# Decoding all float64 weight chunks by way of a PSUM bank, earlier, in a kernel whose order a planner writes

## The chip, the cores and the metric

One core of one Trainium2 chip runs the kernel. The metric is the device time of one launch in microseconds (us). Matmuls run on TensorE (PE), whose clock is granted at one of two levels, 1.2 or 2.4 GHz; VectorE (DVE), ScalarE (ACT) and GpSimd (POOL) do the rest; SyncE (SP) issues all transfers.

## The reference

Causal attention with a decay bias, then two layers of which the first takes a maximum over three projections and the second applies a rational function:

```python
scores = scale * q @ k.T            # 4 batches x 8 heads, 576 positions, 64 wide
bias = -(cum[:, None] - cum[None, :])          # cum: running sum of max(s, 0)
scores = where(causal, -1e9, scores + minimum(bias, 0))
attn = softmax(scores)              # divided by (sum + 1e-9)
x = (attn @ v) as (2304, 512)
h = maximum(maximum(x @ w1, x @ w2), x @ w3)   # 512 -> 768
x = h @ w_out                                  # 768 -> 512
h = x @ w_in2                                  # 512 -> 2048
g = (a0 + a1*h + a2*h^2 + a3*h^3) / (1 + |b0|*|h| + |b1|*h^2 + 1e-6)
return g @ w_out2                              # 2048 -> 512
```

The weights w1, w2, w3, w_out, w_in2 and w_out2 are float64 in memory; the rest is float32.

## The kernel before

Every float32 product is made of three products of float32r halves, so each operand is split into a high part and a remainder (`split`, `minus`: L238 is a copy or cast, L241 a subtract, whatever they work on).

**Attention.** The 32 heads go as 16 pairs (`pr` 0 to 15). For a pair, the K and Q loads (`raw_k`, `raw_q`) are transposed on PE for pairs 0 to 2 (L438) and on DVE after that (`T_k`, `T_q`, L453) and split into `qkT`. `scores` (L502) fills PSUM banks with scores of five row tiles P0 to P4; DVE adds the mask and takes the row minima (L529), ACT the exponentials with their row sums (L537), DVE the reciprocals (`norm`, L555 and L556), and GpSimd or ACT scale the tiles by them (L546, L544). The "flips" (`flip`, L605 and L610) transpose the normalised tiles on PE into banks, which are copied to `PT`; from pair 6 on DVE transposes tile P4 instead (L585) and ACT and GpSimd place it by 16 small copies (`regroup`). `values` (L671) multiplies by V, and the result is split into `x` (cast L238, remainder L684).

**First layer.** When the four pairs of a batch are done, `experts` multiplies its x by w1, w2, w3: 36 "expert groups" a batch, each 12 matmuls of 128x288 on PE (L187) into one bank, and keeps their maximum (`hs`, L797). These groups are the work with which PE is filled while the attention of later pairs waits for other engines. From about 348 us on, PE has only experts and the second layer left (L187, L1022).

**Weights.** A chunk of 128x512 float64 weights (512 KB, `raww`) is turned into float32 on DVE by integer steps (`decode`): L713 shifts the high word, L716 adds the sign, L718 the top bits of the low word. Without `bank` all three write the SBUF tile `wx`; with it the first two work in a bank of PSUM, which L718 reads, and the bank is held from L713 to L718. There are 18 chunks of w1, w2, w3, which are then split into `w13`, 36 of the other weights that are written back to memory as float32 (`spill`), and two that are decoded directly later. Before, the first six go by a bank and 48 of the others by `wx`.

**The order.** Nothing waits for a scheduler on the chip: `Plan` takes every step with a rank, a planned cost on each engine that may do it, its inputs and the banks it takes, and simulates the engines; each time it issues the step that can start first, so the sequence on each engine, and the engine of a step that has a choice (`anyof`), come out of planned times. `SLACK` is added to the planned time of a PE step whose input comes from another engine, from rank 4 on; `wire` plans the transfers.

Of the kernel before, what the change touches and what calls it, by code (L numbers as in the profile page):

```python
# [24 lines left out]
class Plan:  # L25
# [38 lines left out]
    def issue(self):  # L64
        steps = self.steps
        left = [len(s[3]) for s in steps]
        after = [[] for _ in steps]
        for n, s in enumerate(steps):
            for p in s[3]:
                after[p].append(n)  # L70
        end = [0.0] * len(steps)
        est = [0.0] * len(steps)
        engine = {e: self.BEGIN.get(e, 0.0) for s in steps for e in s[0]}
        ready = {e: set() for e in engine}
        for n, s in enumerate(steps):
            if not left[n]:
                for e in s[0]:
                    ready[e].add(n)
        idle = [(0.0, b) for b in self.banks]
        wire = 0.0  # L80
        mode = None
        for _ in steps:
            best = None
            for e, cand in ready.items():
                t = engine[e]
                mine = None
                for n in cand:
                    engs, rank, _, _, take, _, kb, new, price = steps[n]
                    start = max(t, est[n], wire - self.AHEAD if kb else 0.0)
                    if take:  # L90
                        if len(idle) < len(take):
                            continue
                        start = max(start, idle[len(take) - 1][0])
                    if len(engs) > 1 and any(max(engine[o], est[n]) + c * price[o] < start + engs[e] * price[e] for o, c in engs.items() if o != e):
                        continue
                    key = (max(start, t + 0.1), rank + (self.STAY if new and new != mode else 0.0), n)
                    if mine is None or key < mine[0]:
                        mine = (key, start)
                if mine is not None and (best is None or mine[1] < best[0]):
                    best = (mine[1], mine[0][2], e)  # L100
            start, n, e = best
            engs, _, fn, _, take, free, kb, new, _ = steps[n]
            cost = engs[e]
            if new:
                cost += self.TURN if new != mode else 0.0
                mode = new
            for o in engs:
                ready[o].discard(n)
            for h in take:
                h.bank = idle.pop(0)[1]  # L110
            fn(e) if len(engs) > 1 else fn()
            engine[e] = start + cost
            if kb:
                wire = max(wire, start + cost) + kb / (190.0 if wire < 70.0 else 225.0)
                end[n] = wire + 2.0
            else:
                end[n] = start + cost
            lag = self.LAG[e]
            for h in free:
                idle.append((end[n] + lag, h.bank))  # L120
                idle.sort(key=lambda x: x[0])
            for m in after[n]:
                if "ctl" in steps[m][0]:
                    at = start
                else:
                    at = end[n] + ((1.0 if steps[n][1] > 16.0 else 0.0) if kb else self.SAME[e] if list(steps[m][0]) == [e] else lag)
                est[m] = max(est[m], at + (self.SLACK if steps[m][1] > 4.0 and "pe" in steps[m][0] and e not in ("pe", "ctl") else 0.0))
                left[m] -= 1
                if not left[m]:
                    for o in steps[m][0]:  # L130
                        ready[o].add(m)
        return max(end)
# [3 lines left out]
def kernel(  # L136
# [58 lines left out]
    def open_pool(name, **kw):  # L195
        g = tc.tile_pool(name=name, bufs=1, reuse_waits="tile", **kw)
        open_pools[name] = g
        return g.__enter__()
# [17 lines left out]
    def ve(rank, n, fn, reads=(), writes=(), free=(), cost=None):  # L216
        return plan.add({"dve": cost or c_dve(n)}, rank, fn, reads, writes, (), free)
# [13 lines left out]
    def anyof(engs, rank, fn, reads=(), writes=(), free=(), pre=(), price=None):  # L231

        if len(engs) == 1:
            return plan.add(engs, rank, lambda: fn(*engs), reads, writes, (), free, pre=pre)
        return plan.add(engs, rank, fn, reads, writes, (), free, pre=pre, price=price)

    def copy(e, out, in_):
        nc.scalar.copy(out=out, in_=in_) if e == "act" else (nc.vector if e == "dve" else nc.gpsimd).tensor_copy(out, in_)  # L238
# [11 lines left out]
    at = open_pool("at", side="right")  # L250
    n_w = [0]

    def wslot(name, shape=(128, 2, 512)):
        return wp.tile(list(shape), F32R, tag="w", bufs=3 * KF1, name=name)

    def wkey():
        n_w[0] += 1
        return ("w", (n_w[0] - 1) % (3 * KF1))
# [47 lines left out]
    raww = [p1.tile([128, 512, 2], U32, name="raww0"), at.tile([128, 512, 2], U32, name="raww1")]  # L306
    wx = [p1.tile([128, 512], U32, name=f"wx{i}") for i in range(2)]
# [275 lines left out]
    def regroup(pr, rank):  # L583
        for y in range(2):
            ve(rank, 0, lambda y=y: nc.vector.transpose(out=P4[:, :, y], in_=P4[:, :, y]), (), [("P", y, 4)], cost=0.83)  # L585
        for a in range(4):
            for g in range(4):
                anyof({"act": 0.42, "pool": 0.5}, rank + 0.05, lambda e, a=a, g=g: copy(
                    e, PTT[32 * g:32 * g + 32, 1792 + 320 * a:2112 + 320 * a], P[4][32 * a:32 * a + 32, 320 * g:320 * g + 320]),
                      [("P", y, 4) for y in range(2)], [("PT", 8 + 4 * a + g)], (), val[pr - 1] if pr - 1 not in DV else ())  # L590

# [98 lines left out]
    def cols(w, fc):  # L690

        return w.bitcast(U32).rearrange("(k p) f -> p k f", p=128)[:, :, 256 * fc:256 * fc + 256]
# [12 lines left out]
    def decode(rank, raw, x, kraw, kx, bank=False):  # L705


        hold = Hold()

        def way():  # L710
            return hold.bank.bitcast(U32) if bank else x()

        plan.add({"dve": 0.6 if bank else 0.4}, rank, lambda: nc.vector.tensor_scalar(  # L713
            way(), raw()[:, :, 1], 5, 2, ALU.logical_shift_left, ALU.logical_shift_right),
            [kraw], [kx], [hold] if bank else ())
        ve(rank, 0, lambda: nc.vector.scalar_tensor_tensor(  # L716
            way(), raw()[:, :, 1], 0xC0000000, way(), ALU.bitwise_and, ALU.bitwise_or), [kraw], [kx], cost=0.5 if bank else 0.65)
        ve(rank, 0, lambda: nc.vector.scalar_tensor_tensor(  # L718
            x(), raw()[:, :, 0], 29, way(), ALU.logical_shift_right, ALU.bitwise_or), [kraw], [kx],
            [hold] if bank else (), cost=0.5 if bank else 0.65)  # L720
# [21 lines left out]
    def m_rank(b, x):  # L742


        return 4 * b + 4.9 + 4.0 * x / NG
# [5 lines left out]
    def weights():  # L751
        for i in range(3 * KF1):
            fc, m = divmod(i, 3)
            rank = m_rank(0, 6 * fc) - 1.1
            r = raww[i % 2]
            key = w13_key[m, fc] = wkey()

            def new(m=m, fc=fc):
                w13[m, fc] = wslot(f"w13_{fc}_{m}")

            plan.add({"ctl": 0.0}, rank, new, (), [key, "w order"])
            load_raw(rank, r, cols((w1, w2, w3)[m], fc), ("raww", i % 2), e_dma[:4])
            decode(rank, lambda r=r: r, lambda i=i: wx[i % 2], ("raww", i % 2), ("wx", i % 2), i < 6)
            split(rank, lambda i=i: wx[i % 2].bitcast(F32), lambda m=m, fc=fc: w13[m, fc], ("wx", i % 2), key, PR(0 if i < 6 else 9))
        for i, (kind, x) in enumerate(spill):
            rank = S0 + (S1 - S0) * i / len(spill)
            r = raww[i % 2]
            load_raw(rank - 0.3, r, w2_src(kind, x), ("raww", i % 2))
            decode(rank, lambda r=r: r, lambda i=i: wx[i % 2], ("raww", i % 2), ("wx", i % 2))
            dm(rank, 256, w2_dram[i], wx[i % 2].bitcast(F32), [("wx", i % 2)], [("spill", i)])  # L770


# [34 lines left out]
    for pr in range(NP):  # L807
# [12 lines left out]
        if pr in DV:  # L820
            regroup(pr, pr + 0.3)
# [4 lines left out]
        if pr == 0:  # L826
            weights()
# [87 lines left out]
    for i, (_, kind, x) in enumerate(need[:20 + 2 * KF1]):  # L915
        rank = NP + 0.5 + 4.5 * i / 32
# [129 lines left out]
    for c in range(len(chunks) + 4):  # L1046
        n, fc = chunks[min(c, len(chunks) - 1)]
        r = R0 + c
# [49 lines left out]
```

## Time and profile before

| | |
|---|---|
| three timed runs | 891.7 us median (889.71 to 892.25) |
| profiled execution | 893.76 us, of which the span from first to last instruction is 892.0 us |
| busy share of the span | PE 98%, DVE 76%, ACT 60%, GpSimd 44% |
| mean granted clock of PE | 0.99 |

The shares are means over stages with different limits: attention runs until about 348 us, with experts in between, and after that there are matmuls alone. A wait counts only where PE has nothing else to do.

### The profile page before, as it was taken

What the parts mean: (1) busy time and instruction counts of PE and PEld (TensorE: products, weight loads), DVE (VectorE), ACT (ScalarE), POOL (GpSimd) and SP (SyncE); (2) the same over time, 40 slices, a digit from 0 to 9 for tenths busy, and PEclk for the clock granted to TensorE, in tenths of its full rate; (3) what the DMA queues carried; (4) which work ended last, traced back from release to release, by engine and by line L of the source; (5) the groups of instructions that cost most, each with busy time, mean ns of one, the idle gap of its engine ahead of it and who ended that gap; (6) DMA issues with size and microseconds to landing.
All of it is one profiled execution on the core that took longest, in us unless ns stands there. A gap on an engine that the chain in (4) does not pass through costs nothing.

```text
span 892.0 us, 17600 instructions
## 1 busy us (share of the span) xinstructions
PE 872.2 (98%) x6308; PEld 811.2 (91%) x6308; DVE 678.0 (76%) x1488; ACT 532.3 (60%) x1249; POOL 394.9 (44%) x506
## 2 busy tenths in 40 slices
PE   8899899999999999999999999999999999999998
PEld 8789888899999999999999999999999999999997
DVE  8999898878889975764897588478758856874875
ACT  7796476666766654322765576476547647663664
POOL 4465486545444533002853453254335415531432
PEclk9989999999999999999999999999999999999999
DMA  6887757767776754735200010020001002000000
GB/s 167 191 210 195 211 154 210 205 192 220 221 227 195 210 189 152 258 104 146 71 1 1 28 62 1 27 63 1 1 27 64 1 21 68 1 1 1 36 2 35
DMA packets 80664, 93.01 MB, mean 104 GB/s; under 512 B 33792, under 2 KB 61952, under 8 KB 80544
## 3 DMA queue, kind: packets, MB, share of 16 engines
q1 hardware_dynamic: 80576, 91.89, 35.8%
q8 instruction: 49, 0.80, 0.4%
q14 instruction: 39, 0.32, 0.1%
HBM read 69.96 MB, written 21.82 MB: 103 GB/s over the span
## 4 chain that ended last, share of the span: by engine, by line
PE 77%; DVE 8%; POOL 7%; ACT 2%; issue 2%; DMA 2%; SPq 1%; POOLq 0%; DVEq 0%; ACTq 0%
PE bank L187 46%; PE bank L1022 22%; POOL PT L238 4%; PE bank L671 3%; PE bank L610 3%; DVE P L529 2%; PE bank L502 2%; POOL P L546 2%; ACT P L537 1%; DVE P L585 1%; DMA raw_q<-in_q_dram 1%; DVE wx L716 1%; SPq L244 1%; DVE wx L718 1%; PE bank L605 1%
## 5 line engine op out<-in xcount | busy, mean ns | idle before, releaser
L187 PE MATMUL bank<-x,w 128*128 128x288 f32 x1728 | 244.9, 299 | 2.0 <-DVE small L529 2.0
L187 PEld LDWEIGHTS bank<-x,w 128*128 128x128 f32 x1728 | 233.8, 190 | 6.6 <-DVE small L529 2.3
L1022 PE MATMUL bank<-ws,g 128*128 128x512 f32 x864 | 215.5, 393 | 0.0
L187 PE MATMUL bank<-x,ws 128*128 128x384 f32 x1008 | 190.2, 336 | 0.0
L1022 PEld LDWEIGHTS bank<-ws,g 128*128 128x128 f32 x864 | 160.9, 188 | 29.4 <-DVE g L1002 0.2
L187 PEld LDWEIGHTS bank<-x,ws 128*128 128x128 f32 x1008 | 178.2, 188 | 7.1
L978 POOL TENSOR_SCALAR q<-a,cf 128x384 f32<-128x384 f32 x96 | 65.8, 686 | 182.1 <-ACT a L973 181.6
L537 ACT ACTIVATE P<-P,small 128x320 f32<-128x320 f32 (+5 forms) x160 | 89.3, 563 | 25.4 <-DVE small L529 24.8
L980 POOL TENSOR_TENSOR q<-q,a 128x384 f32<-128x384 f32 x96 | 97.8, 1019 | 8.0
L546 POOL TENSOR_SCALAR P<-P,small 128x448 f32<-128x448 f32 (+5 forms) x78 | 57.7, 752 | 96.9 <-ACT P L537 80.0
L995 DVE SCALAR_TENSOR_TENSOR q<-q,cf,bank 128x384 f32<-128x384 f32 x96 | 58.8, 613 | 49.1 <-ACT bank L993 45.9
L241 POOL TENSOR_TENSOR h<-h 128x384 fp32r<-128x384 f32 x30 | 31.1, 1058 | 115.2 <-ACT h L889 100.9
L1001 ACT CAST g<-t 128x384 fp32r<-128x384 f32 x96 | 49.4, 514 | 51.6 <-DVE t L999 51.6
L990 ACT ACTIVATE a<-q,cf 128x384 f32<-128x384 f32 x96 | 59.3, 617 | 28.4 <-POOL q L980 27.4
L187 PE MATMUL bank<-h,ws 128*128 128x384 f32 x432 | 75.9, 336 | 0.0
L187 PEld LDWEIGHTS bank<-h,ws 128*128 128x128 f32 x432 | 75.0, 188 | 0.5
L973 ACT ACTIVATE a<-bank 128x384 f32<-128x384 f32 x96 | 46.9, 489 | 40.8 <-PE bank L187 40.3
L981 DVE TENSOR_TENSOR t<-bank,t 128x384 f32<-128x384 f32 x96 | 53.0, 552 | 21.1 <-ACT t L975 21.1
L797 DVE TENSOR_TENSOR hs<-bank,hs 128x288 f32<-128x288 f32 x96 | 43.1, 449 | 31.3 <-PE bank L187 29.9
L975 ACT ACTIVATE t<-bank,cf 128x384 f32<-128x384 f32 x96 | 64.0, 666 | 0.0
L982 DVE SCALAR_TENSOR_TENSOR t<-t,cf,bank 128x384 f32<-128x384 f32 x96 | 58.8, 613 | 2.4
L999 DVE SCALAR_TENSOR_TENSOR t<-t,cf,bank 128x384 f32<-128x384 f32 x96 | 58.8, 612 | 2.5
(112 smaller groups left out, 1328.8 us busy)
## 6 DMA issues: line engine op xcount, KB each, us to landing
raww<-in_moe_w_out_dram SPq DMA_DIRECT2D x22, 512.0 KB
raww<-in_moe_w_dram SPq DMA_DIRECT2D x18, 512.0 KB
w_dram<-wx SPq DMA_DIRECT2D x36, 256.0 KB
ws<-w_dram SPq DMA_DIRECT2D x36, 256.0 KB
raw_k<-in_k_dram SPq DMA_DIRECT2D x52, 140.0 KB
raw_q<-in_q_dram SPq DMA_DIRECT2D x52, 140.0 KB
raww<-in_moe_w_in_dram SPq DMA_DIRECT2D x14, 512.0 KB
h_dram<-hs SPq DMA_DIRECT2D x48, 144.0 KB
```

What stands on the lines that cost most here:

```text
L187: nc.tensor.matmul(ps, l, r, start=begin and i == 0, stop=end and i == len(seq) - 1)
L537: ac(rank + 0.04, 0, lambda Pi=Pi, m=m, nr=nr: nc.scalar.activation(out=Pi, in_=Pi, func=ACTF.Exp, bias=sm[0:nr, 0, m:m + 1], scale=-1.0, ...
L546: (nc.vector if e == "dve" else nc.gpsimd).tensor_scalar(t, t, c, 0.0, ALU.mult, ALU.add)
L975: ac(rank, 0, lambda: nc.scalar.activation(out=t2[kt], in_=hold.bank[:, 0:TB], func=ACTF.Identity, scale=cf[:, 3:4], bias=cf[:, 2:3]), [(" ...
L978: po(rank, 0, lambda: nc.gpsimd.tensor_scalar(t2[kq], t2[ka], cf[:, 5:6], cf[:, 4:5], ALU.mult, ALU.add), [ka, "cf4"], [kq], cost=0.75)
L980: po(rank, 0, lambda: nc.gpsimd.tensor_tensor(t2[kq], t2[kq], t2[ka], ALU.mult), [ka], [kq], cost=0.97)
L981: ve(rank, TB, lambda: nc.vector.tensor_tensor(t2[kt], hold.bank[:, 0:TB], t2[kt], ALU.mult), [("hp", ci)], [kt])
L982: ve(rank, 0, lambda: nc.vector.scalar_tensor_tensor(t2[kt], t2[kt], cf[:, 1:2], hold.bank[:, 0:TB], ALU.add, ALU.mult), [("hp", ci), ("h ...
L990: ac(rank, 0, lambda: nc.scalar.activation(out=t2[a], in_=t2[qq], func=ACTF.Ln, bias=cf[:, 6:7], scale=1.0), [kq, "cf6"], [ka], cost=0.52)
L995: ve(rank, 0, lambda: nc.vector.scalar_tensor_tensor(t2[qq], t2[qq], cf[:, 6:7], hold.bank[:, 0:TB], ALU.add, ALU.mult), [kr], [kq], cost= ...
L999: ve(rank, 0, lambda: nc.vector.scalar_tensor_tensor(t2[t], t2[t], cf[:, 0:1], hold.bank[:, 0:TB], ALU.add, ALU.mult), [kr, turn], [kt], f ...
L1022: nc.tensor.matmul(hold.bank, t2[kg][:, ga, ts], w2["o2", fc][:, wb, :], start=(fc == 0 and x == 0), stop=(fc == KF2 - 1 and x == 2))
```

## The change

All chunks but the two direct ones are decoded by way of a bank; the chunks of the first layer get a rank 1.6 instead of 1.1 pairs ahead of their use; a PE step that needs a GpSimd result is planned 0.35 us later than one that needs any other; a regroup copy on ACT is planned at 0.47 us instead of 0.42, and the planned rate of transfers rises at 85 us instead of 70.

```diff
--- before.py
+++ after.py
@@ -111,7 +111,7 @@
             fn(e) if len(engs) > 1 else fn()
             engine[e] = start + cost
             if kb:
-                wire = max(wire, start + cost) + kb / (190.0 if wire < 70.0 else 225.0)
+                wire = max(wire, start + cost) + kb / (190.0 if wire < 85.0 else 225.0)
                 end[n] = wire + 2.0
             else:
                 end[n] = start + cost
@@ -124,7 +124,7 @@
                     at = start
                 else:
                     at = end[n] + ((1.0 if steps[n][1] > 16.0 else 0.0) if kb else self.SAME[e] if list(steps[m][0]) == [e] else lag)
-                est[m] = max(est[m], at + (self.SLACK if steps[m][1] > 4.0 and "pe" in steps[m][0] and e not in ("pe", "ctl") else 0.0))
+                est[m] = max(est[m], at + ((self.SLACK + 0.35 if e == "pool" else self.SLACK) if steps[m][1] > 4.0 and "pe" in steps[m][0] and e not in ("pe", "ctl") else 0.0))
                 left[m] -= 1
                 if not left[m]:
                     for o in steps[m][0]:
@@ -585,7 +585,7 @@
             ve(rank, 0, lambda y=y: nc.vector.transpose(out=P4[:, :, y], in_=P4[:, :, y]), (), [("P", y, 4)], cost=0.83)
         for a in range(4):
             for g in range(4):
-                anyof({"act": 0.42, "pool": 0.5}, rank + 0.05, lambda e, a=a, g=g: copy(
+                anyof({"act": 0.47, "pool": 0.5}, rank + 0.05, lambda e, a=a, g=g: copy(
                     e, PTT[32 * g:32 * g + 32, 1792 + 320 * a:2112 + 320 * a], P[4][32 * a:32 * a + 32, 320 * g:320 * g + 320]),
                       [("P", y, 4) for y in range(2)], [("PT", 8 + 4 * a + g)], (), val[pr - 1] if pr - 1 not in DV else ())
 
@@ -751,7 +751,7 @@
     def weights():
         for i in range(3 * KF1):
             fc, m = divmod(i, 3)
-            rank = m_rank(0, 6 * fc) - 1.1
+            rank = m_rank(0, 6 * fc) - 1.6
             r = raww[i % 2]
             key = w13_key[m, fc] = wkey()
 
@@ -760,13 +760,13 @@
 
             plan.add({"ctl": 0.0}, rank, new, (), [key, "w order"])
             load_raw(rank, r, cols((w1, w2, w3)[m], fc), ("raww", i % 2), e_dma[:4])
-            decode(rank, lambda r=r: r, lambda i=i: wx[i % 2], ("raww", i % 2), ("wx", i % 2), i < 6)
+            decode(rank, lambda r=r: r, lambda i=i: wx[i % 2], ("raww", i % 2), ("wx", i % 2), True)
             split(rank, lambda i=i: wx[i % 2].bitcast(F32), lambda m=m, fc=fc: w13[m, fc], ("wx", i % 2), key, PR(0 if i < 6 else 9))
         for i, (kind, x) in enumerate(spill):
             rank = S0 + (S1 - S0) * i / len(spill)
             r = raww[i % 2]
             load_raw(rank - 0.3, r, w2_src(kind, x), ("raww", i % 2))
-            decode(rank, lambda r=r: r, lambda i=i: wx[i % 2], ("raww", i % 2), ("wx", i % 2))
+            decode(rank, lambda r=r: r, lambda i=i: wx[i % 2], ("raww", i % 2), ("wx", i % 2), True)
             dm(rank, 256, w2_dram[i], wx[i % 2].bitcast(F32), [("wx", i % 2)], [("spill", i)])
```

Since planned times decide, the whole order from about 38 us to 345 us moves. Three places of it follow.

On DVE near 40 us, behind the second decode step of the second chunk (`x` is the output of pair 1, `T_k` the transposed K of pair 4, `w` the first chunk's split):

```order
 L716 SCALAR_TENSOR_TENSOR bank_68<-raww_110,bank_68 128x512
-L453 STREAM_TRANSPOSE T_k<-raw_k 128x18x32
-L238 CAST x_126<-bank_73 128x256
+L238 CAST w_0_0_128<-wx_111 128x512
+L718 SCALAR_TENSOR_TENSOR wx_112<-raww_110,bank_68 128x512
+L241 TENSOR_TENSOR w_0_0_128<-wx_111,w_0_0_128 128x512
 L684 TENSOR_TENSOR x_126<-bank_66,x_126 128x320
 L684 TENSOR_TENSOR x_126<-bank_73,x_126 128x256
```

The K transpose moves behind the remainders of x, and work on the first two chunks moves ahead of them.

On DVE, the norm of pair 12 (L555, L556) behind the mask steps of its tile P3, at 266 to 271 us in the profile. Before:

```order
L529 ISA P3_99,small0_102<-bank0_66,mask_86 128x448
L529 ISA small0_102 128x1
L529 ISA P3_99,small0_102<-bank3_69,mask_86 128x448
L529 ISA small0_102 128x1
L529 ISA P4_100,small1_103<-bank5_71,PT_101 128x2x160
L529 ISA small1_103 128x1
L529 ISA P4_100,small1_103<-bank6_72,PT_101 128x2x160
L529 ISA small1_103 128x1
L713 TENSOR_SCALAR wx0_111<-raww0_109 128x512
L555 TENSOR_SCALAR small0_102<-small0_102 128x4
L556 RECIPROCAL small0_102<-small0_102 128x4
```

and with the change:

```order
L529 ISA P3_99,small0_102<-bank1_67,mask_86 128x448
L529 ISA small0_102 128x1
L529 ISA P3_99,small0_102<-bank5_71,mask_86 128x448
L529 ISA small0_102 128x1
L238 CAST qkT0_90<-T_k_93 128x576
L555 TENSOR_SCALAR small0_102<-small0_102 128x4
L556 RECIPROCAL small0_102<-small0_102 128x4
L713 TENSOR_SCALAR bank0_66<-raww1_110 128x512
```

The two mask steps of the next pair (P4) and a first decode step (L713) stood ahead of the norm; now a cast of K does, and L713 stands behind it and writes a bank.

On PE, the first flips of pair 11, at 248 us in the profile, with the last matmul of the expert group ahead of them and the first of the group behind (`w13_4_2` and the like number the groups). Before:

```order
L187 MATMUL bank0_66<-x7_527,w13_4_2_143 128x288
L610 MATMUL bank4_70<-ident_87,P2_98 128x128 x4
L605 MATMUL bank7_73<-ident_87,P2_98 128x128
L605 MATMUL bank7_73<-ident_87,P1_97 128x128
L605 MATMUL bank7_73<-ident_87,P0_96 128x128
L610 MATMUL bank7_73<-ident_87,P1_97 128x128 x2
L187 MATMUL bank3_69<-x4_318,w13_5_0_144 128x288
```

and with the change:

```order
L187 MATMUL bank5_71<-x7_527,w13_5_0_144 128x288
L610 MATMUL bank6_72<-ident_87,P2_98 128x128 x4
L605 MATMUL bank3_69<-ident_87,P2_98 128x128
L605 MATMUL bank3_69<-ident_87,P1_97 128x128
L605 MATMUL bank3_69<-ident_87,P0_96 128x128
L610 MATMUL bank3_69<-ident_87,P1_97 128x128 x2
L187 MATMUL bank1_67<-x4_318,w13_5_1_145 128x288
```

Both orders have the groups 4_1 and 4_2 behind the pair's last scores; group 5_0, which followed the first flips, now runs ahead of them, so three groups instead of two lie between scores and flips.

## Rows read from the trace of the kernel before

**Rows 1.** Busy time by stage: us from and to, then busy us of each engine, PEclk, DMA share, GB/s.
```profile
31.40:57.80 26.40, 23.10 (x237) 19.04 (x235) 24.72 (x81) 20.94 (x65) 14.92 (x20) 0.87 0.97 224
57.80:166.00 108.20, 102.54 (x976) 95.11 (x974) 97.74 (x255) 73.47 (x212) 70.75 (x93) 0.97 0.69 189
166.00:348.50 182.50, 177.80 (x1736) 169.91 (x1736) 148.20 (x381) 112.58 (x319) 89.05 (x131) 0.99 0.69 206
348.50:888.40 539.90, 539.85 (x2932) 501.56 (x2928) 380.32 (x693) 300.42 (x587) 205.31 (x230) 1.00 0.14 43
```

**Rows 2.** What PE waited for: us in total, times, longest us.
```profile
PE bank L610 <- POOL P L546: 7.7, 8, 2.2
PE bank L187 <- DVE small L529: 2.0, 1, 2.0
PE bank L605 <- DVE x L684: 1.5, 1, 1.5
```

**Rows 3.** PE's timeline at three flips: start, us, instructions, idle ahead in brackets.
```profile
92.33 1.97 PE L610 MATMUL bank<-ident,P 128*128 128x128 f32 x8 [2.24 <-POOL P L546]
...
167.00 1.00 PE L610 MATMUL bank<-ident,P 128*128 128x128 f32 x4 [1.58 <-POOL P L546]
168.72 2.68 PE L187 MATMUL bank<-x,w 128*128 128x288 f32 x12
...
198.94 0.66 PE L610 MATMUL bank<-ident,P 128*128 128x128 f32 x4 [0.85 <-POOL P L546]
...
199.90 1.84 PE L187 MATMUL bank<-x,w 128*128 128x288 f32 x12
```

**Rows 4.** DVE's groups by form: count, busy us, mean ns, idle before.
```profile
L713 DVE TENSOR_SCALAR wx<-raww 128x512 uint32<-128x512 uint32 x48 | 27.7, 578 | 3.3 <-POOL w L241 1.7 <-DMA raww<-in_moe_w_in_dram 1.6
L716 DVE SCALAR_TENSOR_TENSOR wx<-raww,wx 128x512 uint32<-128x512 uint32 x48 | 38.2, 795 | 0.7
L718 DVE SCALAR_TENSOR_TENSOR wx<-raww,wx 128x512 uint32<-128x512 uint32 x48 | 37.1, 772 | 0.9
L713 DVE TENSOR_SCALAR bank<-raww 128x512 uint32<-128x512 uint32 x6 | 4.1, 685 | 0.0
L716 DVE SCALAR_TENSOR_TENSOR bank<-raww,bank 128x512 uint32<-128x512 uint32 x6 | 4.1, 688 | 0.1
L718 DVE SCALAR_TENSOR_TENSOR wx<-raww,bank 128x512 uint32<-128x512 uint32 x6 | 4.0, 668 | 0.0
```

**Rows 5.** Timeline of all engines around 268 us.
```profile
268.68 0.18 ACT L537 ACTIVATION_READ_ACCUMULATOR P<-P,small 128x1 f32 x1
268.74 1.43 POOL L241 TENSOR_TENSOR qkT<-T_k,qkT 128x576 fp32r<-128x576 f32 x1
268.76 1.69 DVE L713 TENSOR_SCALAR wx<-raww 128x512 uint32<-128x512 uint32 x1
270.37 0.16 DVE L555 TENSOR_SCALAR small<-small 128x4 f32<-128x4 f32 x1
...
271.77 0.66 PE L610 MATMUL bank<-ident,P 128*128 128x128 f32 x4 [0.66 <-POOL P L546]
```

**Rows 6.** DVE's timeline around 40, 48 and 54 us.
```profile
40.80 1.26 DVE L453 STREAM_TRANSPOSE T_k<-raw_k 128x576 f32<-128x576 f32 x1 [1.47 <-issue]
42.23 0.81 DVE L684 TENSOR_TENSOR x<-bank,x 128x320 fp32r<-128x320 f32 x2
...
48.35 0.69 DVE L238 CAST w<-wx 128x512 fp32r<-128x512 f32 x1
53.72 0.73 DVE L241 TENSOR_TENSOR w<-wx,w 128x512 fp32r<-128x512 f32 x1
```

**Rows 7.** Timeline of DVE and PE around 138 us.
```profile
138.09 1.36 DVE L555 TENSOR_SCALAR small<-small 128x6 f32<-128x6 f32 x1
...
140.24 4.79 PE L187 MATMUL bank<-x,w 128*128 128x288 f32 x24 [2.05 <-DVE small L529]
```

**Rows 8.** Among all waits, PE's weight loads behind the decode.
```profile
PEld bank L502 <- DVE wx L718: 0.5, 3, 0.2
```

## The prediction

> **What bounds the kernel now.** I read the busy time by stage first [rows 1]. From 348.5 us on TensorE (PE) is busy 539.85 of 539.90 us at full clock, and its order from 341 us on is the old one but for the banks. Nothing is to be won or lost there. Before that PE lacks 3.30 us of 26.40 (31.4 to 57.8 us), 5.66 of 108.20 (57.8 to 166) and 4.70 of 182.50 (166 to 348.5). The granted clock adds to this: 0.87, 0.97 and 0.99 in these stages are about 6.9, 6.5 and 3.7 us at the lower level, 1.2 instead of 2.4 GHz (26.40 x 0.13 x 2, and so on); each such us costs at most half a us. So some 13.7 us of idle PE and at most 8.5 us of slow clock can be moved by an edit of the order.
>
> The list of PE's waits [rows 2] says for what. Largest is a flip (a PE transpose of a P tile, L610) that waits for GpSimd's normalisation of that tile (L546): 7.7 us in eight waits. Two are long, 2.24 and 1.58 us; five of 0.66 to 0.86 us come about once a pair from 198 us on ([rows 3] has the two and one of the five, [rows 5] another); the eighth is one of 0.2 at 17 us, ahead of any difference. Behind the two long ones the clock drops: eight flips take 1.62 us from start to start (92.33 to 93.95), where nine take 0.96 later (198.94 to 199.90), and the expert group behind them 2.53 us instead of 1.84. That is 0.77 + 0.69 = 1.5 us; at 167 us it is 0.76 + 0.84 = 1.6 us.
>
> **Why the flips wait.** The rows around 268 us show one case [rows 5]; the order listing of this place stands with the change. ACT has the last row sums at 268.86, so the norm (L555) could run on VectorE (DVE) then. But DVE had two mask steps of the next pair and the first decode step (L713) ahead of it. That L713 takes 1.69 us: it starts 0.02 us after a GpSimd subtract of 1.43 us and ends 0.28 us after it. L555 starts at 270.37, L546 behind it, and the flip at 271.77 has waited 0.66 us. The Trainium skill (SBUF — State Buffer, Who interferes with whom) says that a DVE instruction in a two-port mode, or with two SBUF inputs, and a GpSimd instruction exclude each other for their whole length; the 1.69 us agrees.
>
> **The change, part by part.** *Decode by way of a bank.* [Rows 4]: a chunk costs 578 + 795 + 772 = 2145 ns of DVE now, and 685 + 688 + 668 = 2041 ns where the first six chunks already go by a bank. 48 chunks change: 48 x 0.104 = 5.0 us less DVE. The first step alone gets dearer by 0.107 us, the two others cheaper by 0.107 and 0.104. On the path this counts only where DVE is ahead of PE; DVE idles 10.5 us of 108.2 and 34.3 of 182.5 [rows 1], so I set the direct worth at nothing, with 0 and 5.0 us as bounds. The Trainium skill (VectorE: DVE Perf Modes, Why PSUM operands drop a tier) speaks against this edit: with a PSUM operand fp32 runs at single rate. The first step shows that, the sum of three does not; by the rule alone DVE would carry 48 x 0.107 = 5.1 us more, the bound of a rival below.
>
> *GpSimd results planned later.* In the order of the change three or four expert groups instead of two stand between a pair's scores and its first flip at all five places of a short wait. A group is 1.84 us [rows 3], more than any of the five waits of 0.66 to 0.86 us there. L713 also stands behind the norm now, so the norm comes up to 270.37 - 268.86 = 1.5 us earlier. Either alone covers the waits. **Term 1: 7.7 - 0.2 - 2.24 - 1.58 = 3.7 us gained.** At 167 us three groups now lie before a flip that had none: **term 2: 1.58 + 1.6 = 3.2 us gained.** At 90 us the order is rebuilt (a block of 32 score matmuls now runs before that flip) while DVE is short of time, so I take half of 2.24 + 1.5: **term 3: 1.9 us gained**, bounds 0 and 3.7. ACT's dearer planned copies (0.42 to 0.47) move 8 of 160 regroup copies from ACT to GpSimd, which the 1.5 us covers.
>
> *Chunks 1.6 pairs ahead.* Each of 18 chunks is loaded and decoded half a pair earlier, so its 512 KB transfer passes K and Q loads on SP's queue, and its decode passes the DVE transposes T_k and T_q. At 40 us this helps [rows 6]: DVE stood idle for 1.47 us ahead of T_k, which then ran 1.26, and only behind it came L684 at 42.23, for which a flip waited 1.50 us [rows 2]. Now a cast (0.69), L718 (0.67) and a subtract (0.73) stand there instead of T_k. DVE was free at 40.80 - 1.47 = 39.33, so L684 starts at 41.42. **Term 4: 0.8 us gained**, bounds 0 and 1.5. T_k and T_q come later, but their scores stand a pair further on.
>
> At 140 us an expert group waits 2.05 us for a bank that DVE's mask step frees; ahead of it the tiny L555 took 1.36 us beside a GpSimd subtract [rows 7]. Then 24 matmuls take 4.79 us instead of 2 x 1.84, 1.1 us lost. Of the 32 score matmuls ahead of this group 16 are left there, and two flips follow them first. L555 can still be held up, so I take half of 3.2: **term 5: 1.6 us gained**, bounds 0 and 3.2.
>
> *What is late next.* The order is new from 57 to 348 us, and a plan that is wrong by a few tenths makes waits of its own. Nothing in the trace shows them; their bounds are 0 and the 5.66 us that the rebuilt stage holds now. I take about half, **term 6: 3.0 us lost**.
>
> The sum: 3.7 + 3.2 + 1.9 + 0.8 + 1.6 - 3.0 = 8.2 us. The profiled execution took 893.8 us (span 892.0), so 885.6 for such a one; the three timed runs have a median of 891.7, 2.1 less, so **883.5 us**.
>
> **The rivals.** A, *all of it and no new waits*: terms 3 to 5 at their upper bounds, and the slow clock at 44 us gone too (at most 3.4): 3.7 + 3.2 + 3.7 + 1.5 + 3.2 + 3.4 = 18.7, so 873. For it speaks that decode and GpSimd no longer collide; against it, that norm, transposes and subtracts still can, as L555 shows [rows 7].
>
> B, *the early waits only change places*: DVE is 94% busy from 31 to 58 us and 90% from there to 166 [rows 1], and earlier decode gives it nothing back there. Then term 1 alone remains: 888.0.
>
> C, *banks become scarce, no change*: each decode now holds one of eight banks from L713 until L718 has run, and PE has to wait for L718 to free it. With six chunks PE's weight loads waited three times for that, 0.5 us in all [rows 8], 0.17 each; if each of 48 chunks cost that, 8.2 us would be lost and the forecast's gain with it: 891.7. The first step's 5.1 us (above) would work the same way, were the other steps no cheaper, but DVE's idle time would hide most of it. Against C: by the order listing only seven of the 54 L713 wait for ACT to have left their bank, and one for PE.
>
> D, *slower*: before 57.8 us PE has no expert work to fill in, and DVE has 1.7 us left of 26.4. Two chunks decoded earlier there, each 2.04 + 0.69 us, would put 5.5 us into the chain of the third and fourth pair, with up to 2.8 us more of slow clock. Less term 1 this is 4.6 us lost: 896.3. It decides once the first expert group starts more than about 4 us later than now, at 57.8. Against it: as much transpose work leaves that stretch as decode enters it (T_k 1.26 for L718 and the subtract, 1.40).
>
> **How the numbers follow.** Two runs differ by up to 0.3% here, 2.7 us, so faster means under 889.0 and slower over 894.4. The forecast (880 to 887) has 0.50, A 0.12, B 0.18, C 0.10, D 0.10. B lies under 889 for three quarters of its chance. Faster: 0.50 + 0.12 + 0.14 = 0.76, and 0.02 of C makes 0.78; same 0.12; slower 0.10. The range leaves out D, most of C and the far half of A: 876.5 to 890.5.
>
> **What would show it.** Right: the five regular waits of L610 for L546 gone from PE's list; L713 at about 0.68 us whatever GpSimd does, L716 and L718 without cases over 1 us; PE short of under 2 us from 166 to 348 us; the first expert group still near 57 us. Wrong: PE waits for L718 or for banks (C), new waits of L187 for weights, L502 for transposed K and Q or L671 for GpSimd's copies (B), or a slow clock of more than 7 us before 58 us (D).

## The result, and the profile after

The changed kernel takes **878.73 us** (median of four runs, 878.46 to 878.92) where the kernel before took 891.98 on the same chip (four runs, 889.71 to 894.58): a ratio of 0.985, interval 0.9823 to 0.9878. The forecast was 883.5 with a range of 876.5 to 890.5. The profiled execution took 878.84 us, its span is 877.0.

First the busy times of the whole span. They split the 15.0 us by which the span shrank (892.0 to 877.0):

```profile
PE 865.8 (99%) x6308; PEld 805.2 (92%) x6308; DVE 670.9 (76%) x1492; ACT 530.2 (60%) x1238; POOL 374.8 (43%) x513
```

PE was busy for 872.2 us before, so it idles 11.2 us now instead of 19.8, 8.6 less, and the same 6308 matmuls take 6.4 us less. At most 5.1 of these 6.4 are the slow clock of [rows 1] behind 57.8 us, which is gone. Where the idle time went is seen in the busy time by stage, columns as in [rows 1]:

```profile
31.40:57.80 26.40, 23.52 (x245) 18.98 (x242) 25.63 (x83) 20.77 (x65) 15.45 (x20) 0.87 1.01 227
57.80:166.00 108.20, 107.44 (x1044) 99.61 (x1043) 97.73 (x264) 77.59 (x216) 67.14 (x97) 1.00 0.79 213
166.00:348.50 182.50, 182.50 (x1793) 175.62 (x1792) 149.35 (x390) 110.57 (x310) 72.44 (x134) 1.00 0.72 211
```

PE is short of 0.76 us from 57.8 to 166 us (5.66 before) and of nothing from 166 to 348.5 (4.70 before), at full clock (2.4 GHz). The stretch before 57.8 is nearly as it was (short of 2.88 us, 3.30 before), with the same clock of 0.87. GpSimd (the last "(x...)" column) is busy 16.6 us less in the third stage (89.05 to 72.44) with three instructions more. What PE still waits for answers to [rows 2]:

```profile
PE bank L610 <- ACT P L544: 2.3, 2, 1.8
PE bank L671 <- DMA v<-in_v_dram: 1.4, 1, 1.4
PE bank L187 <- DVE wx L718: 0.6, 1, 0.6
PE bank L610 <- POOL P L546: 0.2, 1, 0.2
```

7.7 us of flips waiting for GpSimd became 0.2. The decode, by form, answers to [rows 4]:

```profile
L716 DVE SCALAR_TENSOR_TENSOR bank<-raww,bank 128x512 uint32<-128x512 uint32 x54 | 37.4, 692 | 0.7
L713 DVE TENSOR_SCALAR bank<-raww 128x512 uint32<-128x512 uint32 x54 | 37.2, 689 | 6.0 <-DMA raww<-in_moe_w_in_dram 3.2 <-DMA raww<-in_moe_w_out_dram 2.8
L718 DVE SCALAR_TENSOR_TENSOR wx<-raww,bank 128x512 uint32<-128x512 uint32 x54 | 36.8, 682 | 1.3
```

A chunk takes 692 + 689 + 682 = 2063 ns, close to the forecast 2041; the longest of the 162 steps is 0.752 us, where one had taken 1.69 [rows 5].

### The profile page after: what moved, and what is told of

It is laid out like the page before. It is cut to its first block, busy times and chain, and to the rows that moved or that the text cites. A ratio compares the mean times of both kernels' runs of the same rounds, so it can differ in the third digit from the quotient of the medians.

```text
span 877.0 us, 17614 instructions
## 1 busy us (share of the span) xinstructions
PE 865.8 (99%) x6308; PEld 805.2 (92%) x6308; DVE 670.9 (76%) x1492; ACT 530.2 (60%) x1238; POOL 374.8 (43%) x513
## 4 chain that ended last, share of the span: by engine, by line
PE 94%; DVE 2%; DMA 1%; POOL 1%; SPq 1%; ACT 1%; issue 0%; POOLq 0%; DVEq 0%
PE bank L187 58%; PE bank L1022 23%; PE bank L502 5%; PE bank L671 5%; PE bank L610 2%; PE bank L605 1%; SPq L244 1%; DMA raw_q<-in_q_dram 1%; DVE P L529 1%; DMA ext_dram<-PT 1%; DVE bank L713 0%; DVE T_q L453 0%; ACT P L537 0%; POOL EXT L361 0%; POOL mask L366 0%
## 5 line engine op out<-in xcount | busy, mean ns | idle before, releaser
L187 PE MATMUL bank<-x,w 128*128 128x288 f32 x1728 | 242.0, 297 | 0.6 <-DVE wx L718 0.6
L187 PEld LDWEIGHTS bank<-x,w 128*128 128x128 f32 x1728 | 230.7, 188 | 5.2 <-issue 1.7
L546 POOL TENSOR_SCALAR P<-P,small 128x320 f32<-128x320 f32 (+5 forms) x77 | 44.2, 589 | 114.3 <-DVE small L556 55.8
```

The costliest lines, as they stand in the source:

```text
L187: nc.tensor.matmul(ps, l, r, start=begin and i == 0, stop=end and i == len(seq) - 1)
```

## The experiments

The question was which edit did it, and by what: the order (waits filled by other work), or the instructions (decode and GpSimd out of each other's way). All runs are against the kernel before on the same chip; its median there was 892.4 us for the first four, 891.83 for the next four, 892.61 for the last. "Over changed" is the median less 878.73; as the chips differ (0.8 us between the medians of before), it is good to about 0.7 us. "Short" is the stage less PE's busy time in the profiled execution, "clock" half of the time at the lower level, worked out from PEclk as in the prediction, and "together" is all three less the changed kernel's 0.76.

| kernel | us (runs from, to) | ratio to before, interval | over changed | short 57.8–166 | short 166–348.5 | clock | together |
|---|---|---|---|---|---|---|---|
| before | 891.98 (889.71, 894.58) | 1 | 13.3 | 5.66 | 4.70 | 5.1 | 14.7 |
| changed | 878.73 (878.46, 878.92) | 0.985 (0.9823, 0.9878) | 0 | 0.76 | 0 | 0 | 0 |
| same order, decode in SBUF | 885.14 (884.29, 886.3) | 0.9921 (0.9902, 0.9941) | 6.4 | 3.62 | 3.55 | 0 | 6.4 |
| bank alone | 881.23 (880.55, 881.59) | 0.9875 (0.9861, 0.989) | 2.5 | 2.72 | 0.86 | 0 | 2.8 |
| 0.35 us alone | 888.18 (887.41, 889.2) | 0.9955 (0.9939, 0.9971) | 9.5 | 6.69 | 1.32 | 2.2 | 9.4 |
| 1.6 pairs alone | 889.56 (888.4, 893.25) | 0.9974 (0.9959, 0.9989) | 10.8 | 4.67 | 4.15 | 0 | 8.1 |
| all but the bank | 885.11 (884.5, 886.13) | 0.9927 (0.991, 0.9945) | 6.4 | 2.76 | 1.42 | 2.2 | 5.6 |
| all but 0.35 us | 881.78 (880.94, 883.15) | 0.9888 (0.9872, 0.9905) | 3.1 | 3.48 | 0 | 0 | 2.7 |
| all but 1.6 pairs | 883.93 (883.1, 884.46) | 0.991 (0.9895, 0.9925) | 5.2 | 3.01 | 0 | 3.2 | 5.5 |
| all but the two planned costs | 882.91 (881.15, 883.87) | 0.9897 (0.9879, 0.9915) | 4.2 | 3.92 | 0.28 | 0 | 3.4 |
| L716, L718 in SBUF | 880.18 (878.99, 880.85) | 0.9869 (0.9843, 0.9896) | 1.5 | 1.97 | 1.72 | 0 | 2.9 |
| spill in SBUF | 883.41 (883.2, 884.76) | 0.991 (0.9884, 0.9936) | 4.7 | 1.80 | 3.80 | 0 | 4.8 |
| 0.35 us for ACT too | 880.26 (880.04, 880.96) | 0.9873 (0.9848, 0.9898) | 1.5 | 2.19 | 0.20 | 0 | 1.6 |
| 1.4 pairs | 879.46 (879.38, 879.72) | 0.9863 (0.9833, 0.9893) | 0.7 | 2.12 | 0 | 0 | 1.4 |

The two columns "over changed" and "together" agree within 1.4 us but for one (10.8 and 8.1). So what PE lacks between 57.8 and 348.5 us, with its clock there, tells most of the time of a version. The start counts in two: flips that the changed kernel starts at 59.48 us start at 61.21 without the 0.35 us and at 60.94 without the two planned costs, and the profiled executions of these two (883.15 and 883.87) are 1.6 us longer than their last column says.

**Same order, decode in SBUF.** The planned costs and held banks of the change stay, so every engine has the changed kernel's order, but 48 chunks are decoded in `wx`:

```diff
-            return hold.bank.bitcast(U32) if bank else x()
+            return hold.bank.bitcast(U32) if bank and wide else x()
...
-            decode(rank, lambda r=r: r, lambda i=i: wx[i % 2], ("raww", i % 2), ("wx", i % 2), True)
+            decode(rank, lambda r=r: r, lambda i=i: wx[i % 2], ("raww", i % 2), ("wx", i % 2), True, i < 6)
```

(`wide` is False for the spilled chunks. `...` marks left-out lines here and below, and a line that breaks off goes on as in the diff of the change.)

> The order of every engine is that of the changed kernel, and the planned banks stay reserved, but 48 of 54 chunks are decoded in the SBUF tile as before. Theory H (the gain comes from decode no longer colliding with GpSimd): the means of the three decode steps go back to about 578, 795 and 772 ns, GpSimd's regroup copies from 453 to about 570 ns, and most of the 13 us gain is lost, 886 to 891 us. Theory O (the gain comes from the order, above all from the third expert group ahead of the flips): the collisions come back too, but PE waits for none of them, and the time stays at 879 to 881 us.

It lost 6.4 of the 13.3 us, between the bands of the two theories. Its busy times, its two stages, and in its list of PE's waits the flips behind GpSimd again:

```profile
PE 865.0 (98%) x6308; PEld 803.8 (91%) x6308; DVE 676.1 (77%) x1492; ACT 528.9 (60%) x1238; POOL 400.4 (45%) x513
```
```profile
57.80:166.00 108.20, 104.58 (x1012) 96.99 (x1013) 99.63 (x258) 75.99 (x215) 76.06 (x93) 1.00 0.77 210
166.00:348.50 182.50, 178.95 (x1756) 170.71 (x1755) 148.31 (x386) 108.53 (x308) 89.13 (x139) 1.00 0.68 201
```
```profile
PE bank L610 <- POOL P L546: 6.5, 8, 1.8
```

The instructions are the same in number and order, yet DVE is busy for 5.2 us more and GpSimd for 25.6 us more. Its decode by form:

```profile
L718 DVE SCALAR_TENSOR_TENSOR wx<-raww,wx 128x512 uint32<-128x512 uint32 x48 | 38.7, 807 | 1.1
L716 DVE SCALAR_TENSOR_TENSOR wx<-raww,wx 128x512 uint32<-128x512 uint32 x48 | 38.5, 801 | 0.7
L713 DVE TENSOR_SCALAR wx<-raww 128x512 uint32<-128x512 uint32 x48 | 25.1, 524 | 3.1 <-DMA raww<-in_moe_w_out_dram 2.1 <-DMA raww<-in_moe_w_in_dram 1.0
```

The whole 3.1 us that DVE idled ahead of L713 are waits for transfers, so it is not that L713 now has to wait for `wx` to come free. GpSimd's groups by form, first of this kernel, then of the changed one:

```profile
L238 POOL COPY PT<-P 32x320 f32<-32x320 f32 x98 | 54.4, 555 | 9.7 <-DVE P L585 4.6 <-PE bank L502 1.1
...
L546 POOL TENSOR_SCALAR P<-P,small 128x448 f32<-128x448 f32 x15 | 14.4, 957 | 0.0
L546 POOL TENSOR_SCALAR P<-P,small 128x320 f32<-128x320 f32 x19 | 14.2, 750 | 9.9 <-DVE small L556 8.3 <-ACT PT L238 0.5 <-PE bank L502 0.5
```
```profile
L238 POOL COPY PT<-P 32x320 f32<-32x320 f32 x98 | 44.4, 453 | 10.8 <-DVE P L585 3.3 <-PE bank L671 1.3 <-PE bank L502 1.3
...
L546 POOL TENSOR_SCALAR P<-P,small 128x320 f32<-128x320 f32 x19 | 10.1, 533 | 12.0 <-DVE small L556 11.3
L546 POOL TENSOR_SCALAR P<-P,small 128x448 f32<-128x448 f32 x15 | 9.6, 641 | 0.0
```

The regroup copies cost GpSimd 10.0 us more, and two of the six forms of L546 8.9 us more. The timelines tell a collision from an instruction that is slow in itself. In the same-order kernel the 36 L716 and L718 on two SBUF operands that no GpSimd instruction overlaps take 0.65 to 0.69 us, and the 60 that one overlaps 0.65 to 1.69, 0.88 on average; the copies take 457 ns on average without a decode step beside them and 631 with one, the 128x448 L546 640 and 1115. In the changed kernel these steps take 0.69 us on average either way, the copies 463 and 448, the L546 642 and 641. How that reaches PE is seen at one flip. The timeline of the same-order kernel around 301 us:

```profile
298.75 2.89 POOL L238 COPY PT<-P 32x320 f32<-32x320 f32 x5
...
300.49 0.82 DVE L716 SCALAR_TENSOR_TENSOR wx<-raww,wx 128x512 uint32<-128x512 uint32 x1
...
301.24 0.42 DVE L555 TENSOR_SCALAR small<-small 128x4 f32<-128x4 f32 x1
...
301.79 0.66 DVE L718 SCALAR_TENSOR_TENSOR wx<-raww,wx 128x512 uint32<-128x512 uint32 x1
...
302.07 2.64 POOL L546 TENSOR_SCALAR P<-P,small 128x320 f32<-128x320 f32 x3 [0.44 <-DVE small L556]
...
302.91 0.44 PE L610 MATMUL bank<-ident,P 128*128 128x128 f32 x2 [1.27 <-POOL P L546]
```

and of the changed kernel at the same instructions:

```profile
292.99 2.44 POOL L238 COPY PT<-P 32x320 f32<-32x320 f32 x5
...
295.33 0.69 DVE L716 SCALAR_TENSOR_TENSOR bank<-raww,bank 128x512 uint32<-128x512 uint32 x1
...
295.93 0.16 DVE L555 TENSOR_SCALAR small<-small 128x4 f32<-128x4 f32 x1
...
296.50 1.65 POOL L546 TENSOR_SCALAR P<-P,small 128x320 f32<-128x320 f32 x3 [1.07 <-DVE small L556]
...
298.02 0.60 PE L610 MATMUL bank<-ident,P 128*128 128x128 f32 x4
```

With the bank the copies, L555 and the normalisation itself are all shorter (2.44 for 2.89, 0.16 for 0.42, 1.65 for 2.64 us), and the flip has no idle time ahead of it. The order alone is thus worth 7.3 us against before (892.4 to 885.14), and what the bank does to the instructions' times, on DVE and GpSimd together, another 6.4.

**Each edit alone.** The kernel before, with the bank for all chunks (in the first layer `i < 6` becomes `True` as well); with the 0.35 us; with the 1.6 pairs:

```diff
-            decode(rank, lambda r=r: r, lambda i=i: wx[i % 2], ("raww", i % 2), ("wx", i % 2))
+            decode(rank, lambda r=r: r, lambda i=i: wx[i % 2], ("raww", i % 2), ("wx", i % 2), True)
```
```diff
-                est[m] = max(est[m], at + (self.SLACK if
+                est[m] = max(est[m], at + ((self.SLACK + 0.35 if e == "pool" else self.SLACK) if
```
```diff
-            rank = m_rank(0, 6 * fc) - 1.1
+            rank = m_rank(0, 6 * fc) - 1.6
```

> The kernel before, with all 54 chunks decoded by a bank and nothing else changed. Theory H: most of the gain, 880 to 884 us, with the decode steps at 0.69 us each and the waits of flips for GpSimd gone although half of the pairs keep two expert groups. Theory O: the order keeps weak places, so 886 to 890 us.

> The kernel before, with GpSimd results planned 0.35 us later and nothing else changed; three groups stand ahead of the flips from pair 9 on. Theory O: the five short waits and the one of 1.58 us with its slow clock are gone, 884 to 886 us, and the decode steps keep their long cases. Theory H: the collisions make other waits, 888 to 892 us.

> The kernel before, with the first-layer chunks ranked 1.6 pairs ahead and nothing else changed. Theory O: the places at 90 and 140 us change, and score blocks of 32 and 16 alternate, 884 to 889 us. Theory H: without a cure of the collisions the earlier decode only moves them, 889 to 894 us.

Against before they win 11.2, 4.2 and 2.8 us (the bank's edit changes the planned order too). The first two came out as theory H had them (880 to 884 and 888 to 892), so theory O's 886 to 890 and 884 to 886 are missed; the third lies just inside theory H's band (889 to 894), with runs down to 888.4. The bank's stages, then its only wait for GpSimd:

```profile
57.80:166.00 108.20, 105.48 (x1023) 97.57 (x1021) 99.74 (x270) 77.45 (x222) 68.58 (x99) 1.00 0.79 208
166.00:348.50 182.50, 181.64 (x1781) 174.58 (x1781) 148.86 (x386) 110.51 (x309) 67.63 (x125) 1.00 0.69 211
```
```profile
PE bank L610 <- POOL P L546: 0.9, 1, 0.9
```

The waits of the 0.35 us alone, and of the 1.6 pairs alone:

```profile
PE bank L610 <- POOL P L546: 5.0, 6, 2.2
PE bank L187 <- DVE small L529: 2.1, 1, 2.1
```
```profile
PE bank L610 <- POOL P L546: 7.5, 12, 1.7
```

The 0.35 us removes most of the short waits from 198 us on, and the long ones at 90, 137 and 165 us stay (2.23, 2.05 and 1.41 us). The 1.6 pairs leaves 0.59 us at 90 us and nothing of the group's wait for a bank at 138, and makes others, of 1.7 us at 139 and 1.34 at 218 among them: twelve waits of flips instead of eight.

**All but one.** The changed kernel with one edit taken back: the bank for all but the first six chunks, the 0.35 us, the 1.6 pairs, or the two planned costs:

```diff
-            decode(rank, lambda r=r: r, lambda i=i: wx[i % 2], ("raww", i % 2), ("wx", i % 2), True)
+            decode(rank, lambda r=r: r, lambda i=i: wx[i % 2], ("raww", i % 2), ("wx", i % 2), i < 6)
```
```diff
-((self.SLACK + 0.35 if e == "pool" else self.SLACK) if
+(self.SLACK if
```
```diff
-            rank = m_rank(0, 6 * fc) - 1.6
+            rank = m_rank(0, 6 * fc) - 1.1
```
```diff
-                wire = max(wire, start + cost) + kb / (190.0 if wire < 85.0 else 225.0)
+                wire = max(wire, start + cost) + kb / (190.0 if wire < 70.0 else 225.0)
...
-                anyof({"act": 0.47, "pool": 0.5},
+                anyof({"act": 0.42, "pool": 0.5},
```

(In the first, the spill's `decode` loses its `True` as well.)

> The changed kernel with only the first six chunks decoded by a bank, as before; the other edits stay. If the collisions of decode and GpSimd carry the part that the order does not (6 us between the changed kernel and the same order decoded in SBUF), it comes to 885 to 888 us, with flips waiting for GpSimd several us in all. If the other edits make a good order by themselves, 880 to 883 us.

> The changed kernel without the 0.35 us for GpSimd results. If the bank route alone keeps the flips from waiting, the time stays within 1 us of the changed kernel, 878 to 880 us. If the third group ahead of the flips is needed as well, short waits for GpSimd come back: 881 to 884 us.

> The changed kernel with the first-layer chunks ranked 1.1 pairs ahead, as before. Bank route alone gave 881.2, so with the GpSimd edit 879.5 to 882 us. If the earlier decode is what fills PE between 57 and 166 us, PE lacks 3 to 5 us there and the time is 882 to 885 us.

> The changed kernel with the two small planned numbers put back (0.42 us for a regroup copy on ACT, transfer rate rising at 70 us). They change no work, only the order: within 1.5 us of the changed kernel, 877.5 to 880.5 us, if a plan near this one is as good as this one; 882 us or more if the order of the changed kernel is a lucky one.

They lose 6.4, 3.1, 5.2 and 4.2 us. The first is within its expectation's first band, the three others within the second: a plan near the changed kernel's is not as good as it, and its order is in part a lucky one. The stage from 57.8 to 166 us in the four, in that order:

```profile
57.80:166.00 108.20, 105.44 (x1005) 96.81 (x1002) 99.05 (x253) 72.47 (x206) 70.44 (x86) 0.98 0.75 205
```
```profile
57.80:166.00 108.20, 104.72 (x1010) 96.09 (x1010) 97.64 (x264) 75.20 (x209) 73.70 (x109) 1.00 0.80 208
```
```profile
57.80:166.00 108.20, 105.19 (x993) 97.39 (x992) 97.79 (x261) 73.64 (x208) 69.68 (x105) 0.97 0.74 203
```
```profile
57.80:166.00 108.20, 104.28 (x1007) 95.67 (x1006) 95.45 (x259) 73.52 (x207) 64.46 (x91) 1.00 0.79 213
```

All four are short there by 2.8 to 3.9 us, the last of them by an edit that only changes two planned numbers. Behind 166 us the three with the bank are full (at most 0.28 short), with the 0.35 us or without it.

**Which step, and where.** Two more kernels in the changed kernel's own order. In one only L713 writes the bank, while L716 writes `wx` and L718 reads two operands in SBUF; in the other the 18 first-layer chunks go by a bank and the 36 spilled ones by SBUF:

```diff
-            way(), raw()[:, :, 1], 0xC0000000, way(), ALU.bitwise_and, ALU.bitwise_or), [kraw], [kx], cost=0.5 if bank else 0.65)
+            way(True), raw()[:, :, 1], 0xC0000000, way(), ALU.bitwise_and, ALU.bitwise_or), [kraw], [kx], cost=0.5 if bank else 0.65)
...
-            x(), raw()[:, :, 0], 29, way(), ALU.logical_shift_right, ALU.bitwise_or), [kraw], [kx],
+            x(), raw()[:, :, 0], 29, way(True), ALU.logical_shift_right, ALU.bitwise_or), [kraw], [kx],
```

(`way(True)` is `x()` from the seventh chunk on; the other kernel has the first diff's `wide` False for the spill alone.)

> Order of the changed kernel, the same on every engine. In 48 chunks only L713 still writes the bank; L716 reads raw words and the bank and writes wx, and L718 reads two operands from SBUF and writes wx. So only one of the three steps can collide with GpSimd by two SBUF inputs, and none by a two-port mode. Theory 1, the first step was what held GpSimd and the norm up: the time stays within 1 us of the changed kernel, 878 to 880, L610 waits for L546 under 1 us in all. Theory 2, each of the three steps had its share of the 6.4 us: a third of it comes back, 880 to 882.5, and L718 has a mean near 0.80 us, as with all in SBUF, with cases over 1 us, while L716 stays near 0.69.

> Order of the changed kernel, the same on every engine. The 18 first-layer chunks go by a bank, the 36 spilled chunks by SBUF. With all 48 in SBUF in this order PE's busy time was 2.9 us less from 57.8 to 166 us and 3.6 us less from 166 to 348.5. Theory 1, each collision costs where it happens: only the later stage loses, 878.7 + 3.6 = 882.3, bounds 881 to 884, with the gaps at flips behind 166 us back. Theory 2, the earlier stage, where VectorE has least to spare, carries the loss on: 879 to 880, as PE has expert groups to fill in with later.

With L718 alone on two SBUF operands 1.5 of the 6.4 us are lost, which the intervals (0.9843 to 0.9896 and 0.9823 to 0.9878) do not tell from nothing. Its waits of flips for GpSimd, its decode and its regroup copies by form:

```profile
PE bank L610 <- POOL P L546: 2.3, 3, 1.2
```
```profile
L718 DVE SCALAR_TENSOR_TENSOR wx<-raww,wx 128x512 uint32<-128x512 uint32 x48 | 37.9, 789 | 1.1
...
L716 DVE SCALAR_TENSOR_TENSOR wx<-raww,bank 128x512 uint32<-128x512 uint32 x48 | 32.5, 676 | 0.8
```
```profile
L238 POOL COPY PT<-P 32x320 f32<-32x320 f32 x98 | 48.7, 497 | 10.0 <-DVE P L585 3.8 <-PE bank L671 1.3 <-PE bank L187 0.7
```

L718, with two operands in SBUF, is at 789 ns again, and L716, which reads one and writes SBUF, stays at 676: in these two it is the second SBUF operand that goes with the longer time, not the output. The copies lie between (497; 453 and 555). The flips' 2.3 us, where the first theory had under 1, and the time favour the second theory: L718 has a share. That each of the other two steps has one is not shown, since no run takes L713 and L716 apart, and the runs reach down into the first theory's band (878.99).

With the spill in SBUF 4.7 us are lost, about the spilled chunks' share of the 48 (36 of 48, of 6.4, is 4.8), and 3.8 us of it show behind 166 us, where most of those chunks are (the first at 137 us): the loss stays where the collision is, as the first theory had it, and later expert groups don't make it good.

```profile
166.00:348.50 182.50, 178.70 (x1753) 170.62 (x1754) 147.06 (x383) 109.33 (x308) 87.40 (x135) 1.00 0.69 203
```

**A better version?** Two more draws of the order: the 0.35 us for ACT's results too, and 1.4 pairs.

```diff
-                est[m] = max(est[m], at + ((self.SLACK + 0.35 if e == "pool"
+                est[m] = max(est[m], at + ((self.SLACK + 0.35 if e in ("pool", "act")
```
```diff
-            rank = m_rank(0, 6 * fc) - 1.6
+            rank = m_rank(0, 6 * fc) - 1.4
```

> The changed kernel with the 0.35 us also added for a PE step that needs a result of ScalarE (ACT). The changed kernel's longest waits left are a flip of 1.80 us for ACT's normalisation at 44 us, where no expert work is there to be moved in, and nothing over 0.7 us later. Theory 1, nothing is left there to win, and a new order is only another draw: 879 to 884, new waits of 1 to 4 us in all before 166 us. Theory 2, planning PE later is good in itself: 877 or less.

> The changed kernel with first-layer chunks 1.4 instead of 1.6 pairs ahead (1.1 cost 5.2 us). Theory 1, the exact figure only draws one order of many, most of which have some waits between 57 and 166 us: 880 to 884, not between the two by rule. Theory 2, the time falls steadily as chunks come earlier: 878.7 + 5.2 x 0.2/0.5 = 880.8, the same place (137 to 141 us) short by a part of what 1.1 lost there.

Neither beats the changed kernel: 880.26 and 879.46. The first is in its first theory's band, another draw. At 1.4 pairs both theories put the time later than it came (880 to 884, 880.8); of the 2.95 us of waits that 1.1 pairs had around 140 us it keeps 0.41, so most of the step's worth is there by 1.4. The wait of L605 for L684 is back, 1.9 us at 41 us, in a version that is 0.7 us longer in all, which its interval does not tell from nothing.

## Why the prediction held, and where it was off

*What bounds it* held: the gain came from PE's waits for GpSimd and DVE and the slow clock behind them, between 57.8 and 348.5 us, and nothing behind that moved.

*Direct worth of the bank, nothing.* This is the step that failed. DVE's saving was sized about right (5.2 us in the same order), but the step priced one side of the collision only. In the changed order GpSimd gets 25.6 us back as well, and it does what the flips wait for. Both together are 6.4 us of kernel time in the same order, outside the step's bounds of 0 and 5.0. No run parts the two engines' shares; at the flip of 301 us GpSimd's two stretches are 1.44 us shorter and DVE's L555 0.26. The prediction quoted the rule on GpSimd and DVE excluding each other (Trainium skill, SBUF — State Buffer, Who interferes with whom) beside L713's 1.69 us, and then used it for DVE's time alone. The runs bear it out for the other steps too: in the changed order L718 takes 789 to 815 ns with two SBUF operands, with one 682. The norm still collides: its L555 takes up to 1.15 us in the changed kernel, at 188.6 us, but no flip waits there.

The sum had the right waits and credited their end mostly to the planned order. Of the edits by themselves the bank is worth 11.2 us, the 0.35 us 4.2 and the 1.6 pairs 2.8. The sum was 4.8 us too small (terms 3 and 5 by 3.4 us, term 6 by 2.2, less the 0.8 of term 4), all but one error to the same side. That the time still lies in the range is owed to the range's width of 14 us, and in part to a lucky order (term 6), not to the mechanism alone.

*Term 1, 3.7 us, and "either alone covers the waits"* held in the main: the five waits are gone here, and the 0.35 us or the bank alone leaves 1.32 or 0.86 us short behind 166 us, of 4.70. *Term 2, 3.2 us* came whole; the 0.35 us alone left 1.41 us of it, the bank alone nothing.

*Terms 3 and 5* were halved (1.9 and 1.6) and came whole (3.7 and 3.2): no wait of over 0.1 us is left behind 76 us. The 0.35 us alone leaves both places waiting; the 1.6 pairs alone leaves 0.59 us of the first and puts a flip's wait of 1.7 us at 139 us in place of the second; the bank alone clears the first and leaves 1.5 us of waits at 137 to 139 us. The second place took the 1.6 pairs together with another edit: from 137 to 142 us the changed kernel without the bank waits 0.12 us, without the 0.35 us not at all, and without the 1.6 pairs 2.95.

*Term 4, 0.8 us* gave nothing. L684 does start earlier, at 41.20 us (forecast 41.42), and its flip waits no more. But the next flip waits 1.80 us for ACT, and those at 59 us start at 59.48 us, where they started at 59.34 before. The changed kernel's timeline there:

```profile
41.20 0.81 DVE L684 TENSOR_TENSOR x<-bank,x 128x320 fp32r<-128x320 f32 x2
...
44.85 1.34 ACT L544 ACTIVATE P<-P,small 128x576 f32<-128x576 f32 x2
...
45.69 1.67 PE L610 MATMUL bank<-ident,P 128*128 128x128 f32 x11 [1.80 <-ACT P L544]
```

*Term 6, 3.0 us lost*, was the largest error of one term: 0.76 us came. It was half of what the stage held before, on the ground that a new plan is wrong somewhere. The other versions show that this is what a new plan mostly costs (2.1 to 3.9 us short from 57.8 to 166 us in every other order that has most of the change), so the size was fair for an order drawn at random, and this order is the best of those tried, which nothing in the prediction gave reason to expect. In its own order 1.2 to 1.4 us of waits stand at 57 us where the clock ahead is higher (last section), so 0.76 flatters it a little.

With what came, the sum is 3.7 + 3.2 + 3.7 + 0 + 3.2 - 0.76 = 13.0 us; the medians differ by 13.3, the profiled executions by 14.9, of which 1.9 have no place in these terms.

*The rivals.* B's 888.0 is about what the 0.35 us alone gives (888.18): most of term 1, and the early waits stay. C shows once, 0.6 us at 75 us; D not at all: the first expert group starts at 57.10 us. A's 873 took the start to win as well, and that did not move.

## What to carry to other kernels

When two engines hold each other up, price both: the one that is off the path in your sum may be the one that the bound engine waits for. An edit's price in time and its effect on a planned order are told apart by a kernel that keeps the order and takes only the instruction back. Versions that differ only in planned numbers spread over 5 us here (879 to 884), so one such number says little until its neighbours have run.

## What the hardware showed besides

**A slow clock that costs little.** In the same order and with the same wait of 1.80 us for ACT ahead, the changed kernel's clock is 0.87 from 31.4 to 57.8 us and the same-order kernel's is 1.00:

```profile
31.40:57.80 26.40, 23.17 (x273) 19.17 (x269) 26.05 (x85) 21.28 (x68) 15.50 (x20) 1.00 1.04 233
```

The two kernels are alike instruction for instruction up to 72 us, where the first decode step in SBUF stands in one. So that wait alone does not decide the clock. With about 6.9 us at the lower level, some 3.4 us of PE's time, the next flips behind 57 us start 0.56 us later, since the kernel at full clock waits there instead. First the changed kernel's flips, then the same-order kernel's, then those of the kernel with the spill in SBUF, alike up to 137 us and also at a clock of 1.00:

```profile
59.48 1.42 PE L610 MATMUL bank<-ident,P 128*128 128x128 f32 x11
```
```profile
58.92 1.42 PE L610 MATMUL bank<-ident,P 128*128 128x128 f32 x11 [1.39 <-POOL P L546]
```
```profile
58.80 1.42 PE L610 MATMUL bank<-ident,P 128*128 128x128 f32 x11 [1.37 <-POOL P L546]
```

The changed kernel's four runs agree: mean clocks of 0.996, 1.000, 0.997 and 0.998 over the whole span go with 878.84, 878.46, 878.62 and 878.92 us. The prediction's "at most half a us for each us of slow clock" was right as a bound, and far from the cost here, where PE would have waited instead.
